# Sliding-window attention with sinks, then a gated feed-forward layer: the attention work of head pairs 9 to 16 goes to TensorE in five bursts for two pairs

## The chip, the cores and the metric

The kernel runs on one core of a Trainium2 chip. The metric is device time in microseconds (us), the median of 13 runs. Nothing is fetched or put in order on the host.

## What is computed

There are 4 batches of 8 heads, 768 tokens and 64 channels per head. A query sees the 128 keys up to itself and the first 4 keys (the sinks). The heads of a batch are laid side by side (512 columns) and go through a gated layer with 1536 hidden columns.

```python
scores = q @ k.T / sqrt(64)                      # per batch and head
keep   = (key < 4) | (0 <= query - key < 128)
a      = exp(scores) where keep, else 0
x      = (a / a.sum(-1)) @ v                     # -> (3072 tokens, 512)
out    = (relu(x @ w_gate) * (x @ w_val)) @ w_out
```

## The kernel before

**Units.** A unit is one pair of heads of one batch: 16 units, four to a batch, numbered 0 to 15. The two heads lie in the two halves of the 128 partitions. Keys are cut in seven blocks of 124 behind a copy of the four sinks, and a block meets only the queries that can see it (`GROUPS`, three groups of up to 503 query columns per head).

For a unit there are these pieces of TensorE work:

- `T`: transposes of k and q with the identity (units 0 to 7). From unit 8 on `X` does it: a DMA transpose on SP's queue, one for k and one for q. `sinkk` then copies the sinks' keys on DVE into `kTs` (L161, L162).
- `S(gi)`, scores of group gi (L181): four or six matmuls, in which the heads use 64 rows of the array each. ScalarE (ACT) takes the exponential out of PSUM into `ee` (L185) and DVE multiplies with the mask (L187). In batch 0 a bias matmul stands in for the mask (L176).
- `V(part)`, for 384 queries: sums of the exponentials (matmuls with `ones`) and then outputs (with `vn`), both at L206, in which the heads use 64 columns of the array each. `norm` calls it and has DVE take the reciprocal of the sums in four instructions (L275, L276, L278, L280), of which the last writes `xT`, the input of the feed-forward layer.

So a score matmul is listed in the profile as 64\*128, an output matmul as 128\*64, and everything else as 128\*128. I call these the three shapes of the array.

**The feed-forward layer** is cut in 96 chunks: batch, half h of its tokens (384), and 128 hidden columns m. A chunk has four matmuls `gp` (L290), ReLU on ACT into `gs` (L293), four matmuls `vp` (L296), and the product `hT` on DVE (L298). After a chunk up to three matmuls of the last product, `op` (L310), are taken from a list `f2`; ACT copies a finished `op` to `ot` (L314) and SP stores it. Chunks are numbered ci = 0 to 95; batch 0 has 0 to 23, and from there on a batch's first half comes before its second.

**PSUM.** `gp`, `vp` and, before the first chunk, the outputs share three banks (`ps_gv`). Scores and outputs share two tiles of two banks in turn (`ps_at`). `op` has one bank.

**Order.** The order of all work is written by hand. The attention work is a list of `stages`, and `PLAN` gives how many of them must have been issued before chunk ci, with straight lines between its points. The stages of a unit up to 7 are six: `S(0)`, `V` of the unit before (part 1), `S(1)`, `t`, `S(2)`, `V` part 0. From unit 8 on they are three bursts: V of the unit before with S(0), then S(1), then V part 0 with S(2). `t` holds the transposes or `sinkk` of the next unit and all that looks ahead: loads of unit x+3 on SP (`held`, whose one-element memset at L346 makes SP's load wait for DVE), the casts of unit x+3 on POOL (GpSimd; L126, L129, L130), and the loads of the weights, which POOL issues too (L225 for `wg` and `wv`, a quarter at a time; L229 for `wo`). An engine takes its instructions strictly in this order.

The two lines of the order that the change bears on most:

```python
PLAN = ((0, 28), (24, 50), (48, 62), (71, 74))
return [both(v, s(0)), both(t, s(1)), both(v0, s(2))] if x >= 8 else [s(0), v, s(1), t, s(2), v0]
```

Of the kernel before, what the change touches and what calls it, by code (L numbers as in the profile page):

```python
# [10 lines left out]
BF16 = mybir.dt.bfloat16  # L11
# [22 lines left out]
def kernel(  # L34
# [12 lines left out]
    nc = tc.nc  # L47
    B, H, S, D = q.shape
    assert (B, H, S, D) == (4, 8, 768, 64)
    NP = H // 2  # L50
# [8 lines left out]
    xpool = ctx.enter_context(tc.tile_pool(name="xp", bufs=2))  # L59
# [18 lines left out]
    wg = const.tile([128, KO, d_ff], BF16, name="wg")  # L78
    wv = const.tile([128, KO, d_ff], BF16, name="wv")
# [10 lines left out]
    class Unit:  # L90
# [3 lines left out]
        def __init__(self, i):  # L94
            self.i, self.b, self.p, self.s = i, i // NP, i % NP, i % 2
            self.kn, self.qn, self.vn, self.stg = kn[i % 3], qn[i % 3], vn[i % 4], stg[i % 4]
            self.xbar = self.b>1
            self.biased = self.b == 0

        def staging(self, x):  # L100
# [118 lines left out]
            nc.tensor.matmul(out=warm_ps[0][:, 0:128], lhsT=ident[:], rhs=ident[:], start=True, stop=True,  # L219
                             skip_group_check=True)  # L220

    def load_w(c):
        n = d_ff // 4
        for w, dst in ((moe_w_gate, wg), (moe_w_val, wv)):
            nc.gpsimd.dma_start(out=dst[:, :, c * n:(c + 1) * n],  # L225
                                in_=w.rearrange("(ko ki) n -> ki ko n", ki=128)[:, :, c * n:(c + 1) * n])

    def load_wo(c):
        nc.gpsimd.dma_start(out=wo[:, 4 * c:4 * c + 4, :],  # L229
                            in_=moe_w_out.rearrange("(ko ki) n -> ki ko n", ki=128)[:, 4 * c:4 * c + 4, :])  # L230
# [12 lines left out]
    def setup_slot(s):  # L243
        nc.vector.memset(kT[s][:, S:872], 0.0)
# [20 lines left out]
    xTs = {}  # L265
    ready = {}

    def norm(u, part, pool=ps_at):

        c0, w, _ = PARTS[part]  # L270
        nb = w // 32
        o, sums = u.V(part, pool)
        r = rpool.tile([128, 2, 384], F32, name="R")
        rc = dpool.tile([128, 12], F32, name="rc")
        nc.vector.transpose(r[:, 0, 0:w], sums[:, 0:w])  # L275
        nc.vector.reciprocal(rc[:, 0:nb], r[:, 0, 0:w].rearrange("p (b j) -> p b j", j=32)[:, :, 0])  # L276
        a = rc[:, 0:nb]
        nc.vector.transpose(r[:, 1, 0:w], bass.AP(a.tensor, a.offset, [a.ap[0], [1, nb], [0, 32]]))  # L278
        ready[u.b, u.p] = c0 + w
        nc.vector.tensor_tensor(xTs[u.b][:, u.p, c0:c0 + w], o[:, 0:w], r[:, 1, 0:w], op=Alu.mult)  # L280
# [37 lines left out]
    with tc.manual_schedule():  # L318
        U = [Unit(i) for i in range(B * NP)]
        on_array = []  # L320

        def at(x):
            return U[x] if 0 <= x < len(U) else None

        def casts(u, what, eng=nc.gpsimd):
            for w in what:
                u.cast(w, eng)

        def load_t(b):
# [12 lines left out]

        def held(x):

            if x < len(U):
                nc.vector.memset(U[x].stg[0:1, 0:1], 0.0)  # L346
                load(x)

        for y in ("k0", "q0", "k1", "q1", "v1", "t", "k2", "q2", "v2", "k3", "q3", "v3"):
            if y == "t":  # L350
                load_t(0)
            elif y[0] in "kq":
                U[int(y[1])].load_kq(y[0], nc.sync)
            else:
                for h in (0, 1) if y[0] == "v" else ("ab".index(y[0]),):
                    U[int(y[1])].load_v(nc.sync, h)
        nc.vector.memset(ones[:], 1.0)
        setup_pool()
        setup_m0()
        nc.scalar.activation(ee[0][:, 0, 0, 0:64], ones[:], Act.Exp, bias=0.0, scale=1.0)  # L360
        for h in range(2):
            U[0].load_v(nc.scalar, h)
        for x in range(2):
            nc.vector.memset(v6[x][:], 0.0)
        setup_slot(0)
        setup_slot(1)
        warm(36)
        casts(U[0], "k", nc.vector)
        casts(U[0], "q", nc.scalar)
        casts(U[1], "kq")  # L370
        casts(U[0], "v")
        cast_t(0)
        casts(U[1], "v")
        casts(U[2], "kqv")
        load(4)


        stages = []

        def unit_stages(x):  # L380
            u, prev, nxt = U[x], at(x - 1), at(x + 1)

            def s(gi):
                def f():
                    if gi == 0 and u.p == 0:
                        xTs[u.b] = xpool.tile([128, NP, S], BF16, name="xT")
                    if gi == 0 and nxt is not None and nxt.xbar:
                        nxt.X()
                    u.S(gi)
                    if x == 0 and gi < 2:  # L390
                        warm(5)
                return f

            def v():
                if prev is not None:
                    norm(prev, 1, ps_at if on_array else ps_gv)

            def t():
                if nxt is not None:
                    if not nxt.xbar:  # L400
                        nxt.T(not on_array)
                    nxt.sinkk()
                if x == 3:
                    load(6)
                elif x == 4:
                    load(7)
                elif x >= 5:
                    held(x + 3)
                if 4 <= x < 6:
                    for c in ((0,), (1, 2))[x - 4]:  # L410
                        load_wo(c)
                if at(x + 3) is not None:
                    casts(at(x + 3), "kqv")
                    if (x + 3) % NP == 0:
                        cast_t((x + 3) // NP)
                if x in (0, 1, 3, 4):
                    load_w((0, 1, 1, 2, 3)[x])
                if x == 0:
                    load(5)
            def v0():  # L420
                norm(u, 0, ps_at if on_array else ps_gv)

            def both(f, g):
                return lambda: (f(), g())
            if x < NP:
                return [s(0), v, s(1), t, s(2), v0]
            return [both(v, s(0)), both(t, s(1)), both(v0, s(2))] if x >= 8 else [s(0), v, s(1), t, s(2), v0]

        def first():
            U[0].T(True)  # L430
            U[0].sinkk()
            setup_m1()
        stages.append(first)
        for x in range(len(U)):
            stages += unit_stages(x)
        stages.append(lambda: norm(U[-1], 1))

        si = 0
        f2 = deque()
        total = len(stages)  # L440

        ORDER = [(0, h, m) for g in range(0, FM, 3) for h in range(2) for m in range(g, g + 3)]
        ORDER += [(b, h, m) for b in range(1, B) for h in range(2) for m in range(FM)]
        PLAN = ((0, 28), (24, 50), (48, 62), (71, 74))

        def want(ci):
            for (c0, w0), (c1, w1) in zip(PLAN, PLAN[1:]):
                if ci <= c1:
                    return w0 + (w1 - w0) * (ci - c0) // (c1 - c0)
            return total  # L450
        count = {}
        n = S // 2
        for ci, (b, h, m) in enumerate(ORDER):
            if b not in hTs:
                hTs[b] = hpool.tile([128, FM, S], BF16, name="hT", tag="hT")
            while si < min(total, want(ci)):
                stages[si]()
                si += 1
            if not ci:
                on_array.append(1)  # L460
# [45 lines left out]
```

The softmax here doesn't subtract the row's maximum and nothing guards it: scores larger than these inputs give would overflow.

## Time and profile before

| | us |
|---|---|
| median of 13 runs (lowest to highest) | 260.05 (258.94 to 262.46) |
| the profiled execution: its own time | 260.98 |
| the profiled execution: span of its instructions | 259.2 |
| TensorE matmul (PE) busy | 249.7 (96%) |
| VectorE (DVE) busy | 145.4 (56%) |
| ScalarE (ACT) busy | 115.9 (45%) |
| GpSimd (POOL) busy | 62.2 (24%) |
| first chunk's first matmul | at 29.46 |
| first DMA transpose issued on SP | at 70.14 |
| last attention matmul of unit 15 | at 193.3 |

The span runs from the first instruction to the last; 1.8 us of the execution's own time lie outside it. A busy share is an average over the whole span: TensorE's ends are modelled, so "busy" there includes short times in which nothing new starts. The start of one row against the start of the next says more. TensorE's clock was granted in full (0.999).

### The profile page before, as it was taken

Reading aid. Unit: us, or ns where it says so; the run is one execution under the profiler, and the core shown is the slowest. Engines: PE = TensorE matmul, PEld = TensorE weight load, DVE = VectorE, ACT = ScalarE, POOL = GpSimd, SP = SyncE. Lnnn points to the kernel's source line nnn. Section 1 sums busy time; section 2 is a strip of 40 time slices with the busy share of each in tenths; the row PEclk is TensorE's granted clock in tenths of the full one; section 3 lists DMA queues with packets and bytes.
Section 4 is the critical chain, followed back from the end, with each engine's and each line's share of the span. In section 5 each row is a group of like instructions: output and inputs, shape, how many; then the busy total and the mean of one; then the engine's idle time right before and its main releaser. Section 6 shows DMA issues by size and latency. Waiting matters only on the chain.

```text
span 259.2 us, 5201 instructions
## 1 busy us (share of the span) xinstructions
PE 249.7 (96%) x2046; PEld 143.6 (55%) x2046; DVE 145.4 (56%) x313; ACT 115.9 (45%) x188; POOL 62.2 (24%) x94
## 2 busy tenths in 40 slices
PE   7999699999979999999999999999999999999994
PEld 7556465665545555555555555556555555555443
DVE  2589969977738574756756565756664322322100
ACT  3888655556523444443544444444533332333212
POOL 6678637901534231404040220000000000000000
PEclk9999999999999999999999999999999999999999
DMA  7999998999999947959591961311011001111122
GB/s 215 303 280 239 249 263 190 187 204 196 230 119 219 225 111 147 139 135 145 78 248 47 183 104 42 61 43 40 3 40 40 35 8 40 43 40 40 40 110 96
DMA packets 77320, 33.56 MB, mean 129 GB/s; under 512 B 64368, under 2 KB 74352, under 8 KB 77296
## 3 DMA queue, kind: packets, MB, share of 16 engines
q1 hardware_dynamic: 69920, 28.12, 49.7%
q0 software_dynamic: 5808, 4.72, 12.2%
q10 hardware_dynamic: 1568, 0.39, 0.7%
q8 instruction: 16, 0.26, 0.4%
q14 instruction: 8, 0.07, 0.1%
HBM read 28.51 MB, written 6.29 MB: 134 GB/s over the span
## 4 chain that ended last, share of the span: by engine, by line
PE 72%; DMA 13%; SPq 6%; POOL 4%; issue 2%; ACT 1%; DVE 0%; POOLq 0%; ACTq 0%; DVEq 0%
PE op L310 23%; PE gp L290 19%; PE vp L296 18%; DMA stg<-in_v_dram 10%; PE ops L206 5%; SPq L119 4%; PE sps L181 4%; DMA kT<-kn 2%; DMA stg<-in_q_dram 2%; SPq L111 1%; POOL vn L129 1%; PE sps L176 1%; POOL vn L130 1%; POOL kn L126 1%; POOL wv L225 1%
## 5 line engine op out<-in xcount | busy, mean ns | idle before, releaser
L298 DVE TENSOR_TENSOR hT<-gs,vp 128x384 bf16<-128x384 f32 x96 | 52.8, 550 | 54.5 <-PE vp L296 53.0
L290 PE MATMUL gp<-xT,wg 128*128 128x384 bf16 x384 | 78.5, 327 | 2.3 <-DVE hT L298 1.8
L296 PE MATMUL vp<-xT,wv 128*128 128x384 bf16 x384 | 78.1, 326 | 1.6 <-DMA wv<-in_moe_w_val_dram 1.6
L293 ACT ACTIVATE gs<-gp 128x384 f32<-128x384 f32 x96 | 47.1, 490 | 62.3 <-PE gp L290 61.1
L310 PE MATMUL op<-wo,hT 128*128 128x512 bf16 (+1 forms) x300 | 74.4, 370 | 0.0
L185 ACT ACTIVATE ee<-sps 128x1006 bf16<-128x1006 f32 (+2 forms) x48 | 46.3, 964 | 46.5 <-PE sps L181 46.3
L296 PEld LDWEIGHTS <-wv 128*128 128x128 bf16 x384 | 37.5, 98 | 26.6 <-DMA wv<-in_moe_w_val_dram 1.9
L290 PEld LDWEIGHTS <-wg 128*128 128x128 bf16 x384 | 34.1, 98 | 32.1 <-issue 6.8
L310 PEld LDWEIGHTS <-hT 128*128 128x128 bf16 x300 | 29.3, 98 | 25.1
L187 DVE TENSOR_TENSOR ee<-ee,msk 128x1006 bf16<-128x1006 bf16 (+2 forms) x36 | 25.4, 704 | 11.0 <-ACT ee L185 11.0
L126 POOL CAST kn<-stg 128x768 bf16<-128x768 f32 x15 | 12.8, 853 | 60.9 <-DMA stg<-in_k_dram 60.9
L314 ACT COPY ot<-op 128x512 f32<-128x512 f32 (+1 forms) x25 | 14.2, 568 | 24.5 <-PE op L310 24.5
L275 DVE STREAM_TRANSPOSE R<-ops 128x384 f32<-128x384 f32 x24 | 13.9, 581 | 12.6 <-PE ops L206 12.5
L278 DVE STREAM_TRANSPOSE R<-rc 128x384 f32<-128x384 f32 x32 | 18.5, 578 | 1.1
L280 DVE TENSOR_TENSOR xT<-ops,R 128x384 bf16<-128x384 f32 x32 | 17.8, 557 | 1.7
L206 PEld LDWEIGHTS <-ones 128*64 128x64 bf16 x288 | 12.3, 109 | 10.8 <-issue 10.0
L129 POOL CAST vn<-stg 128x768 bf16<-128x768 f32 x16 | 13.4, 836 | 12.3 <-DMA stg<-in_v_dram 10.0
L126 POOL CAST qn<-stg 128x768 bf16<-128x768 f32 x15 | 13.1, 873 | 13.2 <-DMA stg<-in_q_dram 8.3
L206 PE MATMUL ops<-ee,vn 128*64 128x255 bf16 (+7 forms) x256 | 15.3, 240 | 0.0
L181 PE MATMUL sps<-qT,kT 64*128 64x251 bf16 (+2 forms) x128 | 14.7, 252 | 0.3 <-ACT qT L154 0.2
L181 PEld LDWEIGHTS <-kT 64*128 64x128 bf16 x128 | 6.3, 93 | 12.7 <-issue 10.3
L161 DVE COPY kTs<-kT 128x372 bf16<-128x372 bf16 x16 | 6.9, 430 | 10.3 <-DMA kT<-kn 5.2
(57 smaller groups left out, 141.5 us busy)
## 6 DMA issues: line engine op xcount, KB each, us to landing
stg<-in_k_dram SPq DMA_DIRECT2D x16, 384.0 KB, 5.2
stg<-in_q_dram SPq DMA_DIRECT2D x16, 384.0 KB, 5.7
out_dram<-ot SPq DMA_DIRECT2D x23, 256.0 KB, 2.0
stg<-in_v_dram SPq DMA_DIRECT2D x30, 192.0 KB, 5.5
wg<-in_moe_w_gate_dram POOLq DMA_DIRECT2D x4, 384.0 KB, 7.6
wv<-in_moe_w_val_dram POOLq DMA_DIRECT2D x4, 384.0 KB, 9.7
wo<-in_moe_w_out_dram POOLq DMA_DIRECT2D x3, 512.0 KB, 12.9
stg<-in_v_dram ACTq DMA_DIRECT2D x2, 192.0 KB, 6.7
```

The lines of the kernel that those rows point to most:

```text
L126: cp((self.kn if what == "k" else self.qn)[:], self.staging(what).rearrange("p h (n d) -> p n h d", d=64))
L181: nc.tensor.matmul(out=ps[:, h, c:c + w], lhsT=self.kw(j, r), rhs=qT[s][r, qa:qa + w], start=not self.biased, stop=True, skip_group_check= ...
L185: nc.scalar.activation(x, ps[:, :, 0:c], Act.Exp, bias=0.0, scale=scale)
L187: nc.vector.tensor_tensor(x, x, bc(msk[:, m0:m0 + c], 2), op=Alu.mult)
L206: nc.tensor.matmul(out=ps[1 - what][64 * h:64 * h + 64, qa - q0:qa - q0 + w], lhsT=self.vw(j, h) if what else ones[:], rhs=ee[s][:, gi, h, ...
L278: nc.vector.transpose(r[:, 1, 0:w], bass.AP(a.tensor, a.offset, [a.ap[0], [1, nb], [0, 32]]))
L280: nc.vector.tensor_tensor(xTs[u.b][:, u.p, c0:c0 + w], o[:, 0:w], r[:, 1, 0:w], op=Alu.mult)
L290: nc.tensor.matmul(out=gp[:, 0:n], lhsT=wg[:, ko, m * 128:(m + 1) * 128], rhs=x[:, ko, c0:c0 + n], start=ko == 0, stop=ko == KO - 1)
L293: nc.scalar.activation(gs[:, 0:n], gp[:, 0:n], Act.Relu, bias=0.0, scale=1.0)
L296: nc.tensor.matmul(out=vp[:, 0:n], lhsT=wv[:, ko, m * 128:(m + 1) * 128], rhs=x[:, ko, c0:c0 + n], start=ko == 0, stop=ko == KO - 1)
L298: nc.vector.tensor_tensor(hT[:, m, c0:c0 + n], gs[:, 0:n], vp[:, 0:n], op=Alu.mult)
L310: nc.tensor.matmul(out=op, lhsT=hTs[b][:, m, t * 128:(t + 1) * 128], rhs=wo[:, m, c0:c0 + n], start=m == 0, stop=m == FM - 1)
```

## The change

From unit 8 on, two units x and x+1 share five bursts, each with one kind of matmul (`pair_stages`):

1. S(0), S(1) of x;
2. V of unit x-1, both parts (for x = 8 only part 1), then what looks ahead for x, `sinkk` of x+1;
3. S(2) of x, S(0) of x+1, then the DMA transposes of x+2;
4. V of x, both parts, then what looks ahead for x+1, `sinkk` of x+2;
5. S(1), S(2) of x+1.

The DMA transposes of x+1 are issued ahead of burst 1. A last stage has both parts of V of unit 15. There are 70 stages in place of 74, and `PLAN` follows: (6, 32) is new, so that stages 31 to 38 come up to one chunk later, and the last point is (71, 70).

Three things change ahead of unit 8. Units 0 to 3 issue S(1) before V of the unit before. The body of `t` that looks ahead is now `ahead(x)`. In it the first quarter of `wg` and `wv` (`load_w(0)`) is issued by POOL ahead of the casts of unit 3, where it stood behind them. `xTs` of a batch is taken from its pool at the batch's first `norm`. The rest of the diff (`xbar`, `which`, the split of the casts of unit 2) leaves the order as it was.

```diff
-            self.xbar = self.b>1
+            self.xbar = i>7
...
+        def ahead(x):
+            if x == 3: load(6)
+            elif x == 4: load(7)
+            elif x >= 5: held(x + 3)
+            if 4 <= x < 6:
+                for c in ((0,), (1, 2))[x - 4]: load_wo(c)
+            if x == 0:
+                load_w(0, (1, 1))
+            if at(x + 3) is not None:
+                casts(at(x + 3), "kqv")
+                if (x + 3) % NP == 0: cast_t((x + 3) // NP)
+            if x in (1, 3, 4):
+                load_w((0, 1, 1, 2, 3)[x])
+            if x == 0: load(5)
...
-                if at(x + 3) is not None:
-                    casts(at(x + 3), "kqv")
...
-                if x in (0, 1, 3, 4):
-                    load_w((0, 1, 1, 2, 3)[x])
...
             if x < NP:
-                return [s(0), v, s(1), t, s(2), v0]
-            return [both(v, s(0)), both(t, s(1)), both(v0, s(2))] if x >= 8 else [s(0), v, s(1), t, s(2), v0]
+                return [s(0), s(1), v, t, s(2), v0]
+            return [s(0), v, s(1), t, s(2), v0]
...
+        def pair_stages(x):
+            u, w, nxt = U[x], U[x + 1], at(x + 2)
...
+            first_outs = outs(U[x - 1], 1) if x == 8 else outs(U[x - 1], 0, 1)
+            a = then(scores((u, 0), (u, 1)))
+            a_ = then(first_outs, lambda: ahead(x), w.sinkk)
+            c = then(scores((u, 2), (w, 0)))
+            d = then(outs(u, 0, 1), lambda: ahead(x + 1), lambda: nxt is not None and nxt.sinkk())
+            e = scores((w, 1), (w, 2))
+            first = [then(turn(w), a)] if w.xbar else [a, turn(w)]
+            second = [then(c, turn(nxt))] if nxt is None or nxt.xbar else [c, turn(nxt)]
+            return first + [a_] + second + [d, e]
...
-        for x in range(len(U)):
+        for x in range(8):
             stages += unit_stages(x)
-        stages.append(lambda: norm(U[-1], 1))
+        for x in range(8, len(U), 2):
+            stages += pair_stages(x)
+        stages.append(lambda: (norm(U[-1], 0), norm(U[-1], 1)))
...
-        PLAN = ((0, 28), (24, 50), (48, 62), (71, 74))
+        PLAN = ((0, 28), (6, 32), (24, 50), (48, 62), (71, 70))
```

More of the change, by code (lines that the diff above doesn't have):

```diff
@@ L220, in warm, with load_w @@
                              skip_group_check=True)
-    def load_w(c):
+    def load_w(c, which=(1, 1)):
         n = d_ff // 4
-        for w, dst in ((moe_w_gate, wg), (moe_w_val, wv)):
-            nc.gpsimd.dma_start(out=dst[:, :, c * n:(c + 1) * n],
-                                in_=w.rearrange("(ko ki) n -> ki ko n", ki=128)[:, :, c * n:(c + 1) * n])
+        for w, dst, wanted in ((moe_w_gate, wg, which[0]), (moe_w_val, wv, which[1])):
+            if wanted:
+                nc.gpsimd.dma_start(out=dst[:, :, c * n:(c + 1) * n],
+                                    in_=w.rearrange("(ko ki) n -> ki ko n", ki=128)[:, :, c * n:(c + 1) * n])
     def load_wo(c):
@@ L270, in norm @@
         c0, w, _ = PARTS[part]
+        if u.b not in xTs:
+            xTs[u.b] = xpool.tile([128, NP, S], BF16, name="xT")
         nb = w // 32
@@ L373 @@
         casts(U[1], "v")
-        casts(U[2], "kqv")
+        casts(U[2], "kq")
+        casts(U[2], "v")
         load(4)
         stages = []
+        def ahead(x):
+            if x == 3:
+                load(6)
+            elif x == 4:
+                load(7)
+            elif x >= 5:
+                held(x + 3)
+            if 4 <= x < 6:
+                for c in ((0,), (1, 2))[x - 4]:
+                    load_wo(c)
+            if x == 0:
+                load_w(0, (1, 1))
+            if at(x + 3) is not None:
+                casts(at(x + 3), "kqv")
+                if (x + 3) % NP == 0:
+                    cast_t((x + 3) // NP)
+            if x in (1, 3, 4):
+                load_w((0, 1, 1, 2, 3)[x])
+            if x == 0:
+                load(5)
         def unit_stages(x):
@@ L384, in f @@
                 def f():
-                    if gi == 0 and u.p == 0:
-                        xTs[u.b] = xpool.tile([128, NP, S], BF16, name="xT")
                     if gi == 0 and nxt is not None and nxt.xbar:
@@ L402, in t @@
                     nxt.sinkk()
[L403 to L411, printed above, removed]
-                if at(x + 3) is not None:
-                    casts(at(x + 3), "kqv")
-                    if (x + 3) % NP == 0:
-                        cast_t((x + 3) // NP)
@@ L416, in t @@
-                if x in (0, 1, 3, 4):
-                    load_w((0, 1, 1, 2, 3)[x])
-                if x == 0:
-                    load(5)
+                ahead(x)
             def v0():
                 norm(u, 0, ps_at if on_array else ps_gv)
-            def both(f, g):
-                return lambda: (f(), g())
             if x < NP:
-                return [s(0), v, s(1), t, s(2), v0]
-            return [both(v, s(0)), both(t, s(1)), both(v0, s(2))] if x >= 8 else [s(0), v, s(1), t, s(2), v0]
+                return [s(0), s(1), v, t, s(2), v0]
@@ new lines, in unit_stages, with scores, f, outs @@
+            return [s(0), v, s(1), t, s(2), v0]
+        def pair_stages(x):
+            u, w, nxt = U[x], U[x + 1], at(x + 2)
+            def scores(*what):
+                def f():
+                    for y, gi in what:
+                        y.S(gi)
+                return f
+            def outs(y, *parts):
+                def f():
+                    for part in parts:
+                        norm(y, part)
+                return f
+            def turn(y):
+                def f():
+                    if y is not None:
+                        y.X() if y.xbar else y.T(False)
+                return f
+            def then(*fs):
+                def g():
+                    for f in fs:
+                        f()
+                return g
+            first_outs = outs(U[x - 1], 1) if x == 8 else outs(U[x - 1], 0, 1)
[7 more added lines that the diff above has]
+            return first + [a_] + second + [d, e]
```

## The prediction

> **What bounds the kernel now.** I read the page's busy table first, then a table by stretches, then who waited for whom, then the order of TensorE and DVE rows inside a unit.
>
> ```profile
> PE 249.7 (96%) x2046; PEld 143.6 (55%) x2046; DVE 145.4 (56%) x313; ACT 115.9 (45%) x188; POOL 62.2 (24%) x94
> DMA  7999998999999947959591961311011001111122
> ...
> 29.46:76.43 46.97, 43.64 (x399) 25.70 (x399) 34.71 (x73) 24.16 (x40) 21.25 (x27) 1.00 1.17 204
> 79.80:194.30 114.50, 114.46 (x919) 63.96 (x920) 72.21 (x156) 50.45 (x83) 18.78 (x25) 1.00 0.57 109
> ...
> PE gp L290 <- DVE hT L298: 1.8, 1, 1.8
> PE vp L296 <- DMA wv<-in_moe_w_val_dram: 1.6, 1, 1.6
> DVE kTs L161 <- DMA kT<-kn: 5.2, 2, 5.1
> ```
>
> In the stretches the columns after the length are PE, PEld, DVE, ACT, POOL busy, clock, DMA share and GB/s. From 79.80 on TensorE is busy 114.46 of 114.50 us and waits for nobody: what its own stream loses there comes off the end. Ahead of that the DMA engines are full (share 1.17), and TensorE's last wait ends at 76.43: `gp` waits 1.76 us for a PSUM bank that `hT` frees; DVE had stood 5.1 us before `kTs` of unit 8 for the first DMA transpose, landed at 75.5. So there are two regimes: up to 76.43 the arrival of data, then TensorE.
>
> Inside a unit (start, duration):
>
> ```profile
> 106.78 0.81 PE L310 MATMUL op<-wo,hT 128*128 128x512 bf16 x3
> 107.52 0.53 PE L206 MATMUL ops<-ee,ones 128*64 128x119 bf16 x10
> 107.91 0.50 PE L206 MATMUL ops<-ee,vn 128*64 128x119 bf16 x8
> 108.24 0.18 PE L206 MATMUL ops<-ee,v 128*64 128x20 bf16 x2
> 108.35 0.28 PE L181 MATMUL sps<-qT,kT 64*128 64x255 bf16 x2
> 108.47 0.27 PE L181 MATMUL sps<-qT,kTs 64*128 64x248 bf16 x2
> 108.67 0.82 PE L290 MATMUL gp<-xT,wg 128*128 128x384 bf16 x4
> ...
> 111.93 0.81 PE L310 MATMUL op<-wo,hT 128*128 128x512 bf16 x3
> 112.67 0.28 PE L181 MATMUL sps<-qT,kT 64*128 64x251 bf16 x2
> 112.79 0.27 PE L181 MATMUL sps<-qT,kTs 64*128 64x248 bf16 x2
> 112.99 0.82 PE L290 MATMUL gp<-xT,wg 128*128 128x384 bf16 x4
> ...
> 108.49 0.58 DVE L275 STREAM_TRANSPOSE R<-ops 128x384 f32<-128x384 f32 x1 [0.88 <-PE ops L206]
> 109.98 0.56 DVE L280 TENSOR_TENSOR xT<-ops,R 128x384 bf16<-128x384 f32 x1
> 110.46 0.68 DVE L187 TENSOR_TENSOR ee<-ee,msk 128x1006 bf16<-128x1006 bf16 x1
> ```
>
> A chunk with three `op` takes 1.95 (0.65 each for `gp`, `vp`, `op`). `op` from 106.78 should hand over at 107.43; V starts at 107.52 and `gp` at 108.67, so V part 1 with S(0) costs 1.24. S(1) alone: 112.58 to 112.99, 0.41. V part 0 with S(2) in the same trace: 102.43 to 103.52, 1.09. A unit is 2.74 (check: 14.47 between units less six chunks is 2.77).
>
> **What a change of shape costs.** S(1) has 499 columns per head, heads side by side; a chunk's pace (4 x 384 columns in 0.65) gives 0.21 for them. The other 0.20 is getting into the scores' shape and out again, 0.09 and 0.11. V alone (batch 0) is 0.09 + 0.71 (61.79 to 62.50) for part 0 and 0.09 + 0.83 (65.63 to 66.46) for part 1; 763 columns twice are 0.64, so in and out cost about 0.15.
>
> A rule of the Trainium skill prices this differently. "TensorEngine Tiling (Array Packing)", Key Properties, says that a new tiling mode drains the array, and "TensorE: Matmul & The Clock Gate", Single matmul latency, puts the fixed part of a warm matmul at 398/2.4 = 166 ns. If every change paid all of it, the 24 changes that go (66 from stage 49 on, now 42: counted in the built program's order) would bring 4.0 us. The rows show 0.06 to 0.11 per change, so some 2.1. I take the rows.
>
> **Part 1: five bursts for six.** Out of the rows above:
> - scores (0,1): 0.41 + 0.21 = 0.62; (2,0) and (1,2): 0.59 each; both parts of V: 0.80 + 0.92 - 0.15 = 1.57. A pair: 0.62 + 2 x 0.59 + 2 x 1.57 = 4.94, against 2 x 2.74 = 5.48.
> - Before, from the first `gp` behind V and S(0) of unit 8 (79.80) to the end of attention: 7 x 1.24 + 8 x 1.09 + 8 x 0.41 + 1.16 (the last V, rows 192.39 to 193.46) = 21.84.
> - After, from the same `gp`: pair 8 0.92 + 0.59 + 1.57 + 0.59 = 3.67; three more pairs 14.82; the last two V 1.57; together 20.06. **Saved: 1.78.**
> - The burst in front of that `gp`: S(0), S(1) at 78.5 in place of V, S(0). S(1) needs the PSUM tile that V part 0 of unit 7 holds until its norm ends (79.3, late because DVE stood for the transpose). The same tile held S(0) before until 79.41. So `gp` starts at 79.41 + 0.32 = 79.73 against 79.80: 0.07, where the shapes promised 0.62.
>
> **Part 2: what doubles up behind a burst.** Both norms of a unit now follow each other: V starts at t + 0.09, DVE 0.83 later (102.52 to 103.35), a norm takes 1.97 (108.49 to 110.46): they end at t + 2.9 and t + 4.85. The next scores, two chunks on, start at t + 1.57 + 3.9 = t + 5.5: both PSUM tiles are free. Behind the norms on DVE stand `sinkk` and the memset (0.35) and then `hT` of the next chunk, done at t + 5.75; the `gp` that wants its bank comes at t + 6.1. Margin 0.35. After two scores the two exponentials (0.91 apart) and `gs` on ACT end 2.8 after the burst's start; the `vp` that needs `gs`'s bank comes at 3.2. Nothing waits, by little. When POOL casts at the same time, DVE copies and masks are slower (L161 1.08 at 26.37 against 0.28; a mask 1.02 at 90.85 against 0.59): that eats the margin now and then. Bounds: 0, and 0.4 on each of seven V bursts, 2.8. I take 0.2 in all, near 0, since between 84 and 193 one row of some thirty is so slowed.
>
> **Part 3: DMA transposes.** X of x+2 is issued in burst 3 and wanted by DVE behind the norms of burst 4, over 5 us later; its wait on SP for S(2) of x (0.3) holds only stores of `ot`. X of x+1 goes out at the same stage as now. Loads (`held`) come a stage earlier or at the same one. Cost 0; the cover is the two chunks and two norms between; without them a transpose shows 5.4 (issue 70.14, landed 75.5).
>
> **Part 4: the first quarter of the weights goes ahead of unit 3's casts.** POOL issues it at 17.7 instead of 21.5 (0.88 + 0.76), so casts of k and q of unit 3 are 1.65 later: their transposes on TensorE (19.57, 19.91) shift by 0.6 and 1.1. And the loads share the engines:
>
> ```profile
> q0 software_dynamic: 609, 0.46, 104.8%
> q1 hardware_dynamic: 107, 0.09, 9.6%
> ```
>
> This is the DMA view of 24 to 27 us: POOL's weights (q0) take all but a tenth; in 19 to 23, without them, q1 moved 1.20 MB. "DMA: Bandwidth & Descriptors", Queues, rings and completion order, has each engine go round between queues packet by packet: by that rule the loads of unit 4 would lose half for six us and come 1 to 1.5 late. By the row they nearly stop for the first three and come 2 to 3 late: v of unit 4 (25.06 now) at 27 to 28, transposes of unit 4 at 26 to 28 instead of 24.48. I take the row; the first `gp` then starts at 30 to 31.7 instead of 29.46, but no `vp` waits 1.56 for `wv` at 31.83. By the third chunk TensorE is between 0.5 ahead and 1.5 behind.
>
> Neither is worth anything: either way it meets the wait that ended at 76.43. As much as it is ahead, it waits longer; it can be 1.76 late before it costs. The bytes up to the first transpose are the same and the engines are full but for 42 to 45.5 (74 GB/s), a gap that ends when POOL, behind v of unit 6 (landed 41.0), issues the second half of the weights. `PLAN` puts `t` of unit 5 a chunk later, so loads of unit 8 are asked for up to 2.4 later than 47.98; until 52 q1 moved nothing then anyway and q0 fills the time. Units 0 to 3 have as many changes of shape as before, S(1) ahead of V only moves ACT's copies 0.7 forward. Bounds for the end of the wait at 76.43: 1 earlier (the gap closes), 3.4 later (2.4 of the late request, 1 of a late POOL). I take 0, since the engines have work throughout.
>
> **Sum.** 1.78 + 0.07 - 0.2 = 1.65 off a span of 259.2. The profiled execution took 260.98, 0.9 over the median; its lost time is not in these rows. Off the median of 260.05: **258.4 us**, 0.6% faster.
>
> **The rivals.**
> - *The first transpose lands late* (slower). The late request at `t` of unit 5 and a later v of unit 6 shift its landing by up to 3.4: net 3.4 - 1.65 = 1.75 slower, 261.8. It decides from 2.4 (slower by 0.3% from a landing at 78 or later). For: unit 8's k took 13.7 us to land even so (47.98 to 61.65). Against: same bytes, full engines. 0.12.
> - *DVE behind double norms stops TensorE*: margin 0.35, seven bursts, some 0.25 each: the gain is gone, 259.9. For: DVE slows under POOL's casts. Against: masks after 84 us are even. 0.14.
> - *The gap at 42 closes*: the wait ends 1 earlier, 257.3. 0.07.
> - That bursts don't merge is out: the built order has 36 output matmuls and 8 or 10 score matmuls in a row.
>
> **How the numbers follow.** Main case 0.67, 258.4 (257.6 to 259.2 its own range). The range takes in the early gap and reaches into the rivals: 257.2 to 260.6. About 0.3% (0.8 us) is what a measurement can tell from no change. Faster: main 0.64 + gap 0.07 + a little of the second rival, 0.73. Same: 0.03 + most of the second rival, 0.14. Slower: the first rival and a remnant, 0.13.
>
> **What would show it.** Right: V rows with 36 in a row lasting 1.57 to the next `gp`, two scores 0.6; TensorE without a releaser from 80 on; attention's last row about 1.7 earlier against the `gp` at 76.43. Wrong: `gp` or `sps` waiting on DVE L280 or L298 behind a V burst; the wait of DVE L161 ending well after 75.6; a `gp` that waits for `wg` at the fourth to sixth chunk.

## The result, and the profile after

The changed kernel takes 258.08 us (median of 11 runs, 256.75 to 261.8). The kernel before, run beside it, takes 260.84 (48 runs, 258.94 to 263.68). The ratio is 0.9899, with a 95% interval of 0.9876 to 0.9922: faster by 2.0 to 3.2 us. The ratios here leave out executions over 1.5% above the fastest of their kernel. The profiled execution took 257.50 us, with a span of 255.7 against 259.2.

First the page after: span, the busy line, and the DMA engines' share over 40 slices.

```profile
span 255.7 us, 5208 instructions
PE 247.5 (97%) x2046; PEld 143.9 (56%) x2046; DVE 148.2 (58%) x313; ACT 115.6 (45%) x188; POOL 61.4 (24%) x94
...
DMA  7999999999999699559948712211011101111132
```

TensorE has the same 2046 matmuls and is busy 2.2 us less. In the DMA row the seventh slice, in which the gap at 42 us lay, is a 9 where it was an 8; a 6 is left further on, at 83 to 89 us.

Next the table by stretches: from the first `gp` to the one where chunk 23 starts, and from the start of chunk 24 to that of chunk 72.

```profile
29.57:75.67 46.10, 44.22 (x398) 25.59 (x397) 35.55 (x74) 24.43 (x40) 24.01 (x33) 1.00 1.15 213
78.27:191.92 113.65, 113.65 (x943) 65.63 (x942) 74.02 (x156) 50.59 (x84) 18.56 (x24) 1.00 0.55 108
```

The second row is the heart of it: TensorE is busy in all of the 113.65 us, and the clock was granted in full (1.00, the third figure from the end). Before, chunk 24 started at 79.73 and chunk 72 at 195.41, 115.68 apart. So 2.03 of the 3.47 us by which the span shrank are here. Another 0.76 lies ahead of chunk 23 (76.43 became 75.67), and 0.71 between chunks 23 and 24 (3.30 became 2.60). From chunk 72 to the end it is 63.79 before and 63.81 after.

Now the rows of two bursts inside that stretch, V of a unit and scores (0,1), each with the `gp` behind it (start, duration).

```profile
90.87 0.81 PE L314 MATMUL op<-wo,hT 128*128 128x512 bf16 x3
91.61 0.47 PE L206 MATMUL ops<-ee,ones 128*64 128x255 bf16 x8
91.94 0.45 PE L206 MATMUL ops<-ee,vn 128*64 128x255 bf16 x8
92.24 0.51 PE L206 MATMUL ops<-ee,ones 128*64 128x119 bf16 x10
92.61 0.50 PE L206 MATMUL ops<-ee,vn 128*64 128x119 bf16 x8
92.94 0.18 PE L206 MATMUL ops<-ee,v 128*64 128x20 bf16 x2
93.05 0.82 PE L294 MATMUL gp<-xT,wg 128*128 128x384 bf16 x4
...
100.81 0.81 PE L314 MATMUL op<-wo,hT 128*128 128x512 bf16 x3
101.56 0.28 PE L181 MATMUL sps<-qT,kT 64*128 64x255 bf16 x2
101.67 0.27 PE L181 MATMUL sps<-qT,kTs 64*128 64x248 bf16 x2
101.78 0.27 PE L181 MATMUL sps<-qT,kT 64*128 64x251 bf16 x2
101.89 0.27 PE L181 MATMUL sps<-qT,kTs 64*128 64x248 bf16 x2
102.09 0.82 PE L294 MATMUL gp<-xT,wg 128*128 128x384 bf16 x4
```

Thirty-six output matmuls stand in a row. `op` hands over 0.65 after its start, so V costs 93.05 - 90.87 - 0.65 = 1.53, and two scores cost 102.09 - 100.81 - 0.65 = 0.63. Summed in this way over the stretch, the bursts take 21.84 before and 19.89 after, a saving of 1.95; the direct difference of the two lengths is 2.03. The 0.08 between them lies in the pace of the chunks: one without a burst takes 1.958 before and 1.955 after.

Behind a V burst, DVE (start, duration):

```profile
110.37 0.56 DVE L284 TENSOR_TENSOR xT<-ops,R 128x384 bf16<-128x384 f32 x1
110.86 0.28 DVE L161 COPY kTs<-kT 128x372 bf16<-128x372 bf16 x1
...
111.12 1.01 DVE L302 TENSOR_TENSOR hT<-gs,vp 128x384 bf16<-128x384 f32 x2
```

V started at 106.09. The second norm ends at 110.93; the next scores start at 111.53, 0.60 later. The first of the two `hT` ends at about 111.65, and the `gp` that wants its bank came at 112.1: 0.45 of margin. The list of TensorE's waits is empty from 36 us on.

Last, what DVE waited for from 40 to 80 us (total, times, longest), and the first DMA transpose on SP:

```profile
DVE kTs L161 <- DMA kT<-kn: 1.4, 1, 1.4
```

```profile
69.08 1.77 SPq L135 DMA_TRANSPOSE kT<-kn  x1
```

It was issued 1.06 earlier than before and the wait is 1.4 us in place of 5.1, and `gp` of chunk 23 does not wait for `hT` in this execution. That was not forecast; most of the experiments ask what it is worth.

### The profile page after: what moved, and what is told of

Read it like the earlier page. It is cut to its first block, busy times and chain, and to the rows that moved or that the text cites. A ratio compares the mean times of both kernels' runs of the same rounds, so it can differ in the third digit from the quotient of the medians.

```text
span 255.7 us, 5208 instructions
## 1 busy us (share of the span) xinstructions
PE 247.5 (97%) x2046; PEld 143.9 (56%) x2046; DVE 148.2 (58%) x313; ACT 115.6 (45%) x188; POOL 61.4 (24%) x94
## 4 chain that ended last, share of the span: by engine, by line
PE 86%; DMA 6%; ACT 2%; POOL 2%; DVE 1%; issue 1%; SPq 1%; POOLq 0%; ACTq 0%; DVEq 0%
PE gp L294 26%; PE op L314 24%; PE vp L300 24%; PE ops L206 7%; DMA stg<-in_v_dram 4%; PE sps L181 4%; DMA stg<-in_q_dram 2%; PE tkq L149 1%; ACT ee L185 1%; DVE kTs L161 1%; POOL vn L129 1%; SPq L114 0%; ACT kT L154 0%; PE sps L176 0%; POOL kn L126 0%
## 5 line engine op out<-in xcount | busy, mean ns | idle before, releaser
L302 DVE TENSOR_TENSOR hT<-gs,vp 128x384 bf16<-128x384 f32 x96 | 52.0, 549 | 48.9 <-PE vp L300 47.6
L185 ACT ACTIVATE ee<-sps 128x1006 bf16<-128x1006 f32 (+2 forms) x48 | 44.5, 963 | 17.3 <-PE sps L181 17.3
L187 DVE TENSOR_TENSOR ee<-ee,msk 128x1006 bf16<-128x1006 bf16 (+2 forms) x36 | 26.1, 727 | 17.7 <-ACT ee L185 17.4
L129 POOL CAST vn<-stg 128x768 bf16<-128x768 f32 x16 | 14.1, 880 | 15.6 <-DMA stg<-in_v_dram 7.7
L126 POOL CAST qn<-stg 128x768 bf16<-128x768 f32 x15 | 12.4, 827 | 8.9 <-DMA stg<-in_q_dram 8.0
L181 PE MATMUL sps<-qT,kT 64*128 64x251 bf16 (+2 forms) x128 | 13.6, 250 | 0.0
L206 PE MATMUL ops<-ee,ones 128*64 128x255 bf16 (+8 forms) x216 | 11.9, 236 | 0.0
```

What stands on the lines that cost most here:

```text
L126: cp((self.kn if what == "k" else self.qn)[:], self.staging(what).rearrange("p h (n d) -> p n h d", d=64))
L181: nc.tensor.matmul(out=ps[:, h, c:c + w], lhsT=self.kw(j, r), rhs=qT[s][r, qa:qa + w], start=not self.biased, stop=True, skip_group_check= ...
L185: nc.scalar.activation(x, ps[:, :, 0:c], Act.Exp, bias=0.0, scale=scale)
L187: nc.vector.tensor_tensor(x, x, bc(msk[:, m0:m0 + c], 2), op=Alu.mult)
L206: nc.tensor.matmul(out=ps[1 - what][64 * h:64 * h + 64, qa - q0:qa - q0 + w], lhsT=self.vw(j, h) if what else ones[:], rhs=ee[s][:, gi, h, ...
L302: nc.vector.tensor_tensor(hT[:, m, c0:c0 + n], gs[:, 0:n], vp[:, 0:n], op=Alu.mult)
```

## The experiments

All compute the whole result, and each was timed against the kernel before on the same chip. A table of single profiled executions first, since several readings rest on it (us; "arrival" is the start of chunk 22, ahead of the wait). One execution is not its kernel: that of the weights first alone is the slowest of its 22 (262.42), that of the six stages 1.2 under its median.

| kernel | DVE's wait for the first transpose | arrival | chunk 23 | chunk 24 | 24 to 72 |
|---|---|---|---|---|---|
| before | 5.1 | 71.83 | 76.43 | 79.73 | 115.68 |
| the change | 1.4 | 72.91 | 75.67 | 78.27 | 113.65 |
| shared bursts alone | 4.8 | 71.37 | 75.76 | 79.01 | 113.65 |
| early part alone | 0.2 | 73.56 | 76.32 | 79.52 | 115.69 |
| weights first alone | 4.7 | 73.39 | 77.86 | 81.16 | 115.68 |
| the change, weights as before | 3.4 | 72.93 | 76.34 | 79.59 | 113.66 |
| six stages a unit | | 72.74 | 75.50 | 77.88 | 117.88 |
| shared bursts, unit 8 asked for early | 1.4 | 73.57 | 76.34 | 78.93 | 113.65 |
| the change, unit 8 asked for early | 0.2 | 72.48 | 75.25 | 77.84 | 113.65 |

### The shared bursts alone

The changed kernel with the early part of before:

```diff
-            if x == 0:
-                load_w(0, (1, 1))
...
-            if x in (1, 3, 4):
+            if x in (0, 1, 3, 4):
...
-                return [s(0), s(1), v, t, s(2), v0]
+                return [s(0), v, s(1), t, s(2), v0]
...
-        PLAN = ((0, 28), (6, 32), (24, 50), (48, 62), (71, 70))
+        PLAN = ((0, 28), (24, 50), (48, 62), (71, 70))
```

> The kernel before with the five shared bursts from unit 8 on and nothing else: early order, the first weights and the plan up to chunk 48 as before. Theory A (two gains: bursts, and an earlier start of the part that TensorE bounds): the wait for the first DMA transpose comes back, TensorE's gp of chunk 23 again waits to about 76.4, the burst behind it waits for the PSUM tile of the norm (about 0.5), and only the bursts are left: 1.8 to 2.0 us faster than before, so 0.6 to 0.9 slower than the whole change. Rival B (the bursts are all of it, the early part only shifts waits): 2.6 us faster than before, the same as the whole change.

Measured: 258.36 us (16 runs), ratio 0.9909 (0.9876 to 0.9943), against 260.71. That is as fast as the change, within the intervals, so the bursts alone can be all of the gain. TensorE's rows with an idle time, between 73 and 82 us (in brackets the idle time and what ended it):

```profile
75.76 0.81 PE L294 MATMUL gp<-xT,wg 128*128 128x384 bf16 x4 [1.56 <-DVE hT L302]
78.69 0.28 PE L181 MATMUL sps<-qT,kT 64*128 64x251 bf16 x2 [0.50 <-DVE xT L284]
```

Here both waits of the prediction are to be seen: `gp` of chunk 23 for `hT`, and S(1) for the PSUM tile of the late norm. Chunks 23 to 24 take 3.25, where before took 3.30. And the stretch behind is 113.65, to the hundredth that of the change. The bursts bring 2.03 there whatever lies ahead. Up to chunk 23 this kernel's order of work is that of before, and yet chunk 23 starts at 75.76 in place of 76.43. So two executions of one order can differ by 0.67 at that point.

### The early part alone

Before, with S(1) ahead of V in units 0 to 3, `load_w(0)` ahead of the casts of unit 3, and the later `t`:

```diff
+                if x == 0:
+                    load_w(0)
                 if at(x + 3) is not None:
                     casts(at(x + 3), "kqv")
...
-                if x in (0, 1, 3, 4):
+                if x in (1, 3, 4):
...
-                return [s(0), v, s(1), t, s(2), v0]
+                return [s(0), s(1), v, t, s(2), v0]
...
-        PLAN = ((0, 28), (24, 50), (48, 62), (71, 74))
+        PLAN = ((0, 28), (6, 32), (24, 50), (48, 62), (71, 74))
```

> The kernel before with the early part alone: units 0 to 3 with S(1) ahead of V, first weights ahead of unit 3's casts, the plan's new point (6, 32); from unit 8 on six bursts for two units as before. Theory A: first DMA transpose lands near 73 instead of 75.5, gp of chunk 23 waits for nothing, attention's end about 0.8 us earlier; 0.7 to 0.9 us faster than before. Rival B: 0, within 0.3.

Measured: 261.11 us (22 runs), ratio 1.0016 (0.9992 to 1.0040). The wait at the transpose is gone (0.2 us left of 5.1), and the kernel is no faster. The table tells why: TensorE arrives at chunk 22 at 73.56 in place of 71.83. What it no longer waits at chunk 23 it has lost earlier, among it 1.2 us for `kn` of POOL at a transpose and 1.2 for `qn` of ACT (0.5 before).

### The weights first, alone

Of the last edit only the two places that move `load_w(0)`.

> The kernel before with one part of the early change: the first quarter of the weights issued by POOL ahead of unit 3's casts. Theory A1 (this is what brings the first DMA transpose forward: v of unit 4 is held up, so the second quarter of the weights goes out later and the loads of units 5 to 7 get ahead of it): POOL issues the third quarter about 1 us earlier than 42.85, the transpose lands 1 us or more before 75.5, 0.5 to 0.9 us faster. Rival A2 (the later request for unit 8's loads, from the plan, or the order of units 0 to 3 does it): 0, within 0.3, the transpose within 0.5 of 75.5.

Measured: 260.88 us (22 runs), ratio 1.0017 (0.9991 to 1.0043). The profiled execution issued the second half of the weights at 44.70 and the first DMA transpose at 72.08, later than before (70.14), and chunk 23 came 1.4 later. An earlier first quarter was expected to pull the transpose forward and to bring 0.5 to 0.9; it did neither, in an execution that is the slowest of its kernel. In the median it is worth nothing that can be measured. Two opposite effects lie behind this; the part on the prediction has them.

### The change with the weights where they were

The opposite: the whole change, but for `load_w(0)`, which stands behind the casts of unit 3 again.

> The changed kernel with the first quarter of the weights back behind unit 3's casts; order of units 0 to 3 and the plan as in the change. If the early part is worth nothing in sum (what the two runs of its parts showed: ratios 1.0016 and 1.0017), this is as fast as the change within 0.3%, 0.991 to 0.988 of before. If the weights' place does help once the bursts are shared, it is 0.5 us or more slower than the change, and TensorE waits for wv at the first chunk (1 to 1.6 us) and for DVE behind the first DMA transpose.

Measured: 258.6 us (6 runs), ratio 0.9890 (0.9844 to 0.9936): as fast as the change. The transpose is issued at 69.91 and DVE waits 3.4.

### Six stages for a unit

The price of a change of shape by the other sign: bursts of before taken apart.

```diff
-            return [both(v, s(0)), both(t, s(1)), both(v0, s(2))] if x >= 8 else [s(0), v, s(1), t, s(2), v0]
+            return [s(0), v, s(1), t, s(2), v0]
...
-        PLAN = ((0, 28), (24, 50), (48, 62), (71, 74))
+        PLAN = ((0, 28), (24, 50), (48, 75), (71, 98))
```

> The kernel before with more changes of shape and no other work: from unit 8 on every score and every output burst stands alone (six stages a unit, the plan scaled to 98 stages), which adds 16 bursts. By the rows of before (V alone 0.80 and 0.92, scores alone 0.38 and 0.41 against 1.09 and 1.24 together) each added burst costs 0.09: 1.4 us slower than before. If each change of shape paid a whole warm latency of 166 ns as the page's figure has it, 2.7 us slower. If a change of shape costs nothing and the gain of the five bursts has another source, 0.

Measured: 262.49 us (13 runs), ratio 1.0096 (1.0064 to 1.0129). The interval is 1.7 to 3.4 us slower, so the median alone does not tell the 1.4 of the rows from the 2.7 of the 166 ns per change that the prediction cites; the rows do. V part 0, alone here:

```profile
103.42 0.81 PE L310 MATMUL op<-wo,hT 128*128 128x512 bf16 x3
104.16 0.47 PE L206 MATMUL ops<-ee,ones 128*64 128x255 bf16 x8
104.49 0.45 PE L206 MATMUL ops<-ee,vn 128*64 128x255 bf16 x8
104.87 0.82 PE L290 MATMUL gp<-xT,wg 128*128 128x384 bf16 x4
```

It takes 104.87 - 103.42 - 0.65 = 0.80, and S(2) alone takes 0.38; together, before, they take 1.09. One change of shape is the difference, 0.09. In the same way V part 1 (0.92) and S(0) (0.42) against 1.24 give 0.10, and both parts of V against the 1.53 of the change give 0.19 for two.

The whole agrees with that. Work that stood ahead of chunk 24 in one kernel stands behind it in another, so I count from chunk 23 to chunk 72, where all three hold the same work. Before takes 118.98, the change 116.25, the six stages 120.25. In 118.98 there are 0.35 that neither of the others has: 0.11 in the burst ahead of chunk 24 (1.35 in place of 1.24), where S(0) comes late, at 79.41, and 0.24 in the last V (1.16 in place of 0.92). By the rows that V waits for a mask: it starts while DVE still works on the mask of the last scores.

```profile
192.14 0.58 DVE L187 TENSOR_TENSOR ee<-ee,msk 128x830 bf16<-128x830 bf16 x1
...
192.39 0.75 PE L206 MATMUL ops<-ee,ones 128*64 128x119 bf16 x9
```

The change then saves 2.73 - 0.35 = 2.38 with 24 changes of shape fewer, 0.10 each. The six stages cost 1.27 + 0.35 = 1.62 with 15 more, 0.11 each (16 bursts were cut, but two of the pieces, at 136.29, fell on one chunk and stand together again). Two edits of opposite sign give nearly one price.

### Bursts a chunk apart

The changed kernel, with the bursts of the last units closer together:

```diff
-        PLAN = ((0, 28), (6, 32), (24, 50), (48, 62), (71, 70))
+        PLAN = ((0, 28), (6, 32), (24, 50), (48, 62), (56, 70), (71, 70))
```

> The changed kernel with its last eight stages one chunk apart in place of nearly three (plan point (56, 70)), the work the same. It tests the margin behind the double norms. Theory (a norm takes 1.97, two end 4.85 after a V burst starts, and the scores' second PSUM tile is free only then): with one chunk between, scores come at 3.5, so each V burst that scores follow makes TensorE wait about 1.3 for DVE, three times: 3 to 5 us slower than the change, with sps rows that wait for DVE L284. Rival (the two tiles are not what holds the scores, or DVE works faster than the sum of its rows): no wait, as fast as the change.

Measured: 261.58 us (20 runs), ratio 1.0016 (0.9993 to 1.0040): the gain is gone. Rows of TensorE at one of three such places, and of DVE there:

```profile
155.77 0.47 PE L206 MATMUL ops<-ee,ones 128*64 128x255 bf16 x8
...
159.27 0.28 PE L181 MATMUL sps<-qT,kT 64*128 64x251 bf16 x2
159.39 0.27 PE L181 MATMUL sps<-qT,kTs 64*128 64x248 bf16 x2
160.67 0.28 PE L181 MATMUL sps<-qT,kT 64*128 64x251 bf16 x2 [1.01 <-DVE xT L284]
```

```profile
158.10 0.56 DVE L284 TENSOR_TENSOR xT<-ops,R 128x384 bf16<-128x384 f32 x1
...
160.06 0.56 DVE L284 TENSOR_TENSOR xT<-ops,R 128x384 bf16<-128x384 f32 x1
```

The first scores find a tile that the first norm freed at 158.66. The second scores wait until the second norm has ended at 160.62. At three places a burst of scores then costs 1.8 to 2.0 in place of 0.6. That makes 3.8 in sum, and the stretch is 3.75 longer (117.40 against 113.65). So the second chunk between bursts is what lets the double norms go unseen: without it the change is worth nothing. The loss is real, and in the change it does not occur.

### Loads a unit earlier

On the shared bursts alone: loads of unit 8 and all later ones asked for one unit earlier, to fill the gap at 42 us.

```diff
             elif x == 4:
                 load(7)
+                held(8)
             elif x >= 5:
-                held(x + 3)
+                held(x + 4)
```

> The five shared bursts alone (first run of this study) and one more edit: from unit 8 on a unit's loads are asked for one unit earlier (unit 8's with unit 7's). Theory (the wait for the first DMA transpose is set by the bytes queued ahead of it, and the engines idle from 42 to 45.5 because unit 8's loads are asked for at 48): the gap is filled, the transpose lands before 73, gp of chunk 23 waits for nothing, and with no later part of the early change in the way all 1.6 us of that wait come off: 3.5 to 4.3 us faster than before. Rival (the weights behind that gap are then late by as much): a gp or vp waits for wg or wv at chunk 12 or 18, and it is no faster than the shared bursts alone.

Measured: 263.79 us (9 runs), ratio 1.0097 (1.0059 to 1.0135): a miss. SP's queue, then TensorE:

```profile
71.62 3.80 SPq L119 DMA_DIRECT2D stg<-in_v_dram  x2
75.59 1.30 SPq L135 DMA_TRANSPOSE kT<-kn  x1
```

```profile
79.96 1.44 PE L294 MATMUL gp<-xT,wg 128*128 128x384 bf16 x4 [5.52 <-DVE hT L302]
81.19 1.49 PE L300 MATMUL vp<-xT,wv 128*128 128x384 bf16 x4
...
86.03 0.81 PE L300 MATMUL vp<-xT,wv 128*128 128x384 bf16 x4
```

SP takes its instructions in order. Now one more unit's loads stand ahead of the first transpose there, and it is issued at 75.59 in place of 69.70. `gp` of chunk 23 waits 5.5 us, and then TensorE runs at half pace for 6 us (four matmuls in 1.23 in place of 0.65). From chunk 23 to 24 it takes 4.89, against 3.25 in the same bursts without the early loads: 1.64 more, and 0.52 more behind chunk 24. The table by stretches shows why: the clock, third from the end, was granted by half.

```profile
79.11:85.94 6.83, 5.98 (x23) 2.44 (x23) 4.49 (x12) 1.90 (x3) 1.72 (x3) 0.50 1.00 184
```

### Shared bursts from unit 4 on

The last edit, and two units sharing five bursts from unit 4 on, with a `PLAN` for it:

```diff
-        for x in range(8):
+        for x in range(4):
             stages += unit_stages(x)
-        for x in range(8, len(U), 2):
+        for x in range(4, len(U), 2):
             stages += pair_stages(x)
...
```

> The same with the shared bursts from unit 4 on, transposes of units 5 to 7 on TensorE between bursts. By the rows of before, units 4 to 7 cost 4 x 2.92 in bursts that stand alone, and 2 x 4.94 plus one more entry when shared: 1.5 us less. If TensorE bounds from the third chunk on (no wait left behind it), 1 to 1.5 us faster than the run before this one. If data bound it there, or DVE's double norms meet its casts, 0, with waits of TensorE for DVE or for POOL's casts between 30 and 70.

Measured: 264.55 us (6 runs), ratio 1.0143 (1.0096 to 1.0189). The early loads of the last edit are in it, and with them their loss: the transpose is issued at 75.15, and TensorE waits 5.5 us and then runs at the halved clock.

```profile
79.97 1.44 PE L300 MATMUL vp<-xT,wv 128*128 128x384 bf16 x4 [5.53 <-DVE hT L302]
```

What the bursts from unit 4 on do shows ahead of that. Chunk 22 starts 2.0 later than in the last experiment (73.61 against 71.61): where the data bind, fewer changes of shape brought nothing here, and coarser stages brought longer waits (1.9 for `wv` in place of 1.2, and new ones of 0.7, 0.6 and 0.5).

### Unit 8 alone earlier

The way out of the queue's trap: only unit 8's loads earlier, so that nothing new stands ahead of the transpose. On the shared bursts alone, and on the change.

```diff
             elif x == 4:
                 load(7)
-            elif x >= 5:
+                held(8)
+            elif x >= 6:
                 held(x + 3)
```

> The shared bursts with the early part of before, and the loads of unit 8 alone asked for one unit earlier (in the look-ahead of unit 4, right behind those of unit 7); all later loads as they were, so that nothing new stands ahead of the first DMA transpose on SP's queue. Theory (the first transpose lands late because the DMA engines idle from 42 to 45.5 us and because unit 8's loads are asked for at about 48): the loads fill that gap, SP issues the transpose by 67 to 68 in place of 69.7, DVE's wait for it shrinks from 4.8 to under 2.5, the gp behind it waits under 0.3, and the span is 255.0 to 255.8 against 256.4 for the shared bursts alone: ratio to before 0.984 to 0.987. Rival (bytes: all that the engines carry until 70 us has to pass anyway, and the weights that POOL issues then come as much later): the transpose is issued at 69.5 or later, TensorE waits for weights or as long as before for the transpose, ratio 0.990 to 0.995.

> The changed kernel whole, with the same earlier request for unit 8. It already arrives about 1 us later at chunk 22 and in its profiled execution waited for nothing from 35 us on, so an earlier transpose can bring it nothing: both theories expect the changed kernel's 0.989 to 0.991; the rival of bytes expects 0.991 to 0.996 if the weights come later for it.

Measured: 257.97 us (6 runs), ratio 0.9876 (0.9829 to 0.9922), and 258.21 us (15 runs), ratio 0.9887 (0.9856 to 0.9917), against 261.0. Neither differs from the change. The first has the gap filled (DMA share from 42 to 46 us 1.19, against 0.91 with the shared bursts alone) and DVE's wait down to 1.4 as expected, but the transpose is issued at 70.21, not at 67 to 68, and the span is 256.4, not under 255.8. Its waits of TensorE from 29 to 250 us:

```profile
PE vp L300 <- DMA wv<-in_moe_w_val_dram: 2.0, 1, 2.0
PE gp L294 <- DMA wg<-in_moe_w_gate_dram: 0.3, 1, 0.3
```

The wait of 1.56 at chunk 23 is gone, and waits of 2.3 for the weights stand at the first chunks; with the shared bursts alone that was 0.8. Chunk 24 starts at 78.93 against 79.01. Behind the 2.0 us for `wv` the clock was halved in this execution:

```profile
32.92:36.34 3.42, 3.42 (x20) 2.29 (x19) 1.03 (x2) 0.49 (x1) 0.08 (x1) 0.50 1.21 241
```

Both stand ahead of chunk 22, which starts at 73.57 against 71.37. Four of the six executions kept the full clock, with a median of 257.26. What the early request is worth without the halved clock is not settled by so few.

## Why the prediction was right, and where its terms were off

It forecast 258.4 us out of the bursts, nothing for the early part, and small stalls. The time is 258.08. As a difference it was low: 1.65 forecast, 2.0 to 3.2 measured beside the kernel before, whose median was 260.84 in that comparison against the 260.05 that the forecast started from. So the close time is in part a shift of the starting point, which is luck.

- **Part 1, five bursts for six.** Held, a little low. Forecast 21.84 to 20.06. The rows give 21.84 to 19.89: V of a unit measures 1.53 where 1.57 was taken (eight of them, and -0.3 in sum), the scores 0.59 to 0.63 where 0.59 and 0.62 were taken (+0.1). The weighing of rows against the rule is settled as well. The prediction had 0.06 to 0.11 for a change of shape; the rows give 0.09 to 0.10, the change and the six stages 0.10 and 0.11. With 166 ns for each, 24 changes would have brought 4.0 us; from chunk 23 on the profiles show 2.73, of which 0.35 are waits. The 1.16 that the prediction took for the last V of before was no price of V: 0.24 of it is, by the rows, the wait for a mask, and that went too.
- **The burst ahead of it.** 0.07 was taken, from a `gp` at 79.80 and one at 79.73. But the rows of before have that `gp` at 79.73 already, so the reasoning gives 0. With the shared bursts alone it is 0.05, and the wait of 0.50 for the PSUM tile stands in the rows. In the profiled execution of the change, where the transpose came in time, it is 0.70: the whole 0.62 that "the shapes promised", and the 0.11 that before loses there. The reason given was right; what it hangs on, the transpose's landing, moved.
- **Part 2, doubled norms.** A term that was too large: 0.2 was taken, and none is left, with TensorE's list of waits empty from 36 us on. The times were right (second norm at t + 4.9, `hT` at t + 5.65 against t + 5.75, where t is 106.0). The bursts a chunk apart show that the rival built on it was no idle fear: waits of 1.0 to 1.1 behind a V burst with only one chunk between. It does not come true because two chunks stand there, not because norms are cheap.
- **Part 3, the DMA transposes.** 0, and 0 it is: no wait for `kTs` or `qT` behind 80 us.
- **Part 4, the early part.** The sum of 0 held: 1.0016 (0.9992 to 1.0040) alone. The road to it was half right. The first chunks came later by 0.9 at the third, inside the forecast "0.5 ahead to 1.5 behind", and the wait for `wv` left. Loads of unit 8 were asked for 1.97 later, where 2.4 had been the bound. But the wait at 76.43 was taken to stay where it was. In the profiled execution it went: the gap at 42 us closed, as the third rival had it, and chunk 23 came 0.76 earlier. Of the 3.47 in the span, 1.5 lie ahead of chunk 24.

How much of that 1.5 is the change's own is not settled, but most of it need not be. The two executions are 3.48 apart (260.98 and 257.50), where the medians are 2.76 apart; and the shared bursts alone, with the early order of before, start chunk 23 earlier by 0.67. Of the kernels that reach the transpose in time (waits of 0.2 to 1.4), chunk 23 starts at 75.25 to 76.34; of those that wait for it (3.4 to 5.1), at 75.76 to 77.86. TensorE's own path and the path of the data end within a us of each other there, so taking away the wait of one shows that of the other. The medians of the change, the shared bursts alone and the change with the old weights (ratios 0.9899, 0.9909, 0.9890) cannot be told apart.

The medians hide one effect of the early part: it keeps the clock. Each execution has its mean granted clock on record. That is 0.998 to 1.000 in most of them, and 0.993 or less in the others; 3.4 us at half clock, as in the trace of unit 8 alone earlier, make 0.993 of a whole execution. Among the executions that the ratios keep, profiled ones included (without the two kernels that wait 5.5 us):

| first quarter of the weights | kernels | executions with a loss of clock |
|---|---|---|
| behind the casts of unit 3 | before | 33 of 103 |
| behind them | shared bursts alone, old weights, six stages, unit 8 early on shared bursts | 18 of 41 |
| ahead of them | the change, early part alone, weights first alone, bursts a chunk apart, unit 8 early on the change | 3 of 83 |

The change and the change with the old weights differ in nothing else: 0 of 11 against 3 of 6. On the other side, at full clock the early part alone takes 261.00 and the weights first alone 260.87, where before, beside them, takes 260.13 at full clock and 261.33 with a loss. So with the bursts of before the early weights cost some 0.8 us at full clock, and they spare about a third of the executions some 1.2. In sum nothing is left that can be measured, as forecast, but the prediction had no term for the clock. That the wait for `wv` causes the loss is seen in one trace only; no execution of before with a loss has a profile.

## What to carry to other kernels

Where TensorE has no wait, each change of the array's shape that an order saves came off the end in full here; price it from rows of the kernel itself, by a burst's start and the next start, over a stretch that holds the same work in both kernels, and check the price with an edit of the opposite sign. When bursts are merged, what they release merges too: work out when the second norm ends against the next use of its tile, since one chunk less between bursts cost the whole gain. Where several transfers and a busy engine end at the same point, removing the last wait is no evidence of a gain: look at when the engine arrives there. And where executions of one kernel scatter, sort them by the granted clock first.

## What the runs showed of the hardware

- After a long wait TensorE's clock was halved. With the loads a unit earlier TensorE stood 5.5 us, to 79.96, and the granted clock was 0.50 from 79.11 to 85.94; with shared bursts from unit 4 on it stood 5.5 us, to 79.97, and the clock was 0.50 from 77.08 to 83.90. A wait of 2.0 us was enough too: with unit 8 alone earlier it ended at 31.91, and the clock was 0.50 from 32.92 to 36.34. After the waits of 1.6 and 1.8 in the profiled execution of before the clock stayed full. "TensorE: Matmul & The Clock Gate" of the Trainium skill, part 1, has a clock that halves after an idle window of about 3.4 us and returns after about as long of work. By that the 2.0 us would have cost no more than themselves; in the trace 3.4 us of half clock followed, an estimated 1.7 us of work. For the prediction it means that a late transpose is dearer than its wait. Its first rival, a landing 3.4 us later, would have made TensorE wait about 5.2 us (1.76 + 3.4); after 5.5 us, with the loads a unit earlier, the halved clock cost 2.2 on top (1.64 + 0.52).
- A change of the array's shape cost 0.09 to 0.11 us in merged and split bursts, and the stretch that TensorE bounds repeats to 0.01 us over five kernels with the same bursts (113.65 or 113.66), while chunk 23 moves by over a us between kernels.
